# Loading all raw token weights first and decoding one piece a step, with zeros on TensorE and the cap and first keys moved ahead, in a soft-capped attention and token/channel mixer

## The chip, the cores and the metric

The kernel runs on one core of one Trainium2 chip. The metric is the device time of one execution in microseconds; the median of three runs is given with their range. Profiles show one execution, taken by the hardware profiler. TensorE (PE) multiplies matrices, VectorE (DVE), ScalarE (ACT) and GpSimd (POOL) compute on vectors, and SyncE (SP) issues most DMAs.

## The reference

Two stages: attention with soft-capped scores, then a mixer over tokens and over channels. B, H, S, D = 4, 12, 448, 64.

```python
scores = np.matmul(q, k.transpose(0, 1, 3, 2)) / np.sqrt(64)
scores = cap * np.tanh(scores / cap)
scores = scores - np.max(scores, axis=-1, keepdims=True)
attn = np.exp(scores)
attn = attn / (np.sum(attn, axis=-1, keepdims=True) + 1e-09)
x = np.matmul(attn, v)                      # then (4, 448, 768)
xt = x.transpose(0, 2, 1)
h = np.maximum(xt @ w_tok1, 0.0) @ w_tok2   # over tokens, 448 -> 256 -> 448
u = x + h.transpose(0, 2, 1)
h2 = np.maximum(u @ w_ch1, 0.0) @ w_ch2     # over channels, 768 -> 1536 -> 768
out = u + h2
```

The four weight matrices are float64 on the host and reach the kernel as raw 64-bit words. The kernel decodes them into a high and a low float32 part, and every product with them is made of three matmuls.

## The kernel before

**Attention.** The 12 heads of a batch are six pairs of heads. A pair has three full key chunks of 128 (units c = 0, 1, 2), and the remaining 64 keys of two neighbouring pairs share one packed unit (c = 3). So two pairs make seven units, in the order (p, 0..3), (p+1, 0..2), and the list of all units is worked off two units a step. In a step `scores_of` puts the score matmuls (`qk_unit`, ps_qk, two banks) on TensorE, then two tanh and two exp on ScalarE; the exps go into the tiles e, of which there are eight. Step t of the loop issues on TensorE first the products of probabilities and values of step t (`pv_full`, `pv_packed`, into ps_pv), then the scores of step t + 2. ps_pv has two banks, one a pair: a pair gets its bank with its first product, and when its four products are done, `evac` copies the bank out on VectorE in the next step. The third pair's first product comes in step 3, the fourth pair's in step 5.

VectorE also sums the probabilities: `add_up` adds the e tiles of a pair into acc (`L236`, `L242`, and two half adds `L254`). The column sums of acc go through TensorE (ps_s, L262), a gather, a reciprocal and a broadcast, and `scale_pair` (L300) writes the normalized result to u. `transpose_pair` (ps_t, L323) and the two token products (ps_h, ps_u) are given to TensorE as background work of later steps.

**Order.** Within the attention stage every engine executes its instructions in the order in which the Python code issues them (a manual schedule). `at(d, f, y)` puts off a piece of work by d steps; `run(0)`, `run(1)`, `run(2)` issue it at the beginning, the middle and the end of a step. SyncE's DMAs are in the same order too, and one that waits holds up those behind it.

**Token weights.** w1 comes in two pieces of 512 elements a partition, w2 in two of 448. `decode_steps` gives four closures, and in the first batch each step that contains a unit c = 1 starts one. `decode` issues the load of a piece into one of two wraw tiles; `lag` steps later `first` issues two VectorE operations (L98, L101), a step later `second` two more (L106, L107), then `third` two (L110, L111), and `fourth` a cast to the high part (L115) and a subtraction on GpSimd for the low part (L118).

**Start.** SP loads the first pair's queries, ScalarE's queue loads its keys and then the cap; SP goes on with the second and third pair and the values. Both tanh and exp need a factor that VectorE makes of the cap (L463 to L465).

Of the kernel before, what the change touches and what calls it, by code (L numbers as in the profile page):

```python
# [8 lines left out]
F32 = mybir.dt.float32  # L9
F32R = mybir.dt.float32r  # L10
I32 = mybir.dt.int32
# [4 lines left out]
P = 128  # L16
B, H, S, D = 4, 12, 448, 64
# [5 lines left out]
NK = 4  # L23
NF = NK - 1
NV = 2 * NF + 1
LAST = S - (NK - 1) * P
# [3 lines left out]
DU = 512  # L30
HALF = C // 2
NHALF = NC // 2
SP = 32
FREE = 40.0
EPS = 1e-9


@with_exitstack
def tile_softcap_mixer(ctx, tc, qk, v, cap, w1, w2, wc1, wc2, out):
    nc = tc.nc  # L40

    const = ctx.enter_context(tc.tile_pool(name="const", bufs=1))
    wp = ctx.enter_context(tc.tile_pool(name="wp", bufs=2))
    ps_a = ctx.enter_context(tc.tile_pool(name="ps_a", bufs=2, space=PSUM))
    ps_b = ctx.enter_context(tc.tile_pool(name="ps_b", bufs=2, space=PSUM))
    ps_c = ctx.enter_context(tc.tile_pool(name="ps_c", bufs=2, space=PSUM))

    def bits(ap):
        return ap.bitcast(F32)

    cap_sb = const.tile([P, 1], F32, name="cap_sb")
# [4 lines left out]
    u = [const.tile([P, NC, S], F32, name=f"u{b}") for b in range(B)]  # L56
# [6 lines left out]
    w1s = last_u[:, :n1].rearrange("p (x c t) -> p x c t", x=2, c=NK)  # L63
    w2s = last_u[:, n1:n1 + 2 * NT * S].rearrange("p (x t s) -> p x t s", x=2, t=NT)
# [6 lines left out]
    def at(d, f, y=0):  # L71
        later.setdefault((now[0] + d, y), []).append(f)

    def run(y):
        for f in later.pop((now[0], y), []):
            f()

    def tick(most=3):
        now[0] += 1
        for y in range(most):  # L80
            run(y)
# [4 lines left out]
    pace = [1]  # L86

    def decode(src, n, hi, lo, early, blank):
        r = wp.tile([P, 2 * DU], I32, tag="wraw", name="wraw")[:, :2 * n]
        nc.sync.dma_start(r, src.bitcast(I32))  # L90
        r = r.rearrange("p (n t) -> p n t", t=2)

        z = wp.tile([P, DU], I32, tag="wz", name="wz")[:, :n]
        zf = bits(z)

        def first():
            if early:
                nc.vector.tensor_scalar(  # L98
                    z, r[:, :, 1], 1, 1, op0=ALU.logical_shift_left, op1=ALU.logical_shift_right
                )  # L100
                nc.vector.tensor_scalar_mul(zf, zf, 2.0 ** -16)  # L101
                return
            nc.scalar.activation(zf, bits(r[:, :, 1]), AF.Abs, scale=2.0 ** -16)  # L103

        def second():
            nc.vector.tensor_scalar(zf, zf, 2.0 ** -31, 2.0 - 2.0 ** -23, op0=ALU.max, op1=ALU.min)  # L106
            nc.vector.tensor_scalar(z, z, 4, 1, op0=ALU.logical_shift_left, op1=ALU.logical_shift_right)  # L107

        def third():
            nc.vector.scalar_tensor_tensor(z, r[:, :, 1], -(1 << 31), z, op0=ALU.bitwise_and, op1=ALU.bitwise_or)  # L110
            nc.vector.scalar_tensor_tensor(z, r[:, :, 0], 29, z, op0=ALU.logical_shift_right, op1=ALU.bitwise_or)  # L111

        def fourth():
            if early:
                nc.vector.tensor_copy(hi, zf)  # L115
            else:
                nc.scalar.activation(hi, zf, AF.Copy)  # L117
            nc.gpsimd.tensor_tensor(lo, zf, hi, op=ALU.subtract)  # L118
            if blank is not None:
                nc.gpsimd.memset(bits(blank), 0.0)  # L120

        d = lag[0]
        at(d, first)
        d += slow[0]
        at(d, second, 2)
        at(d + 1, third, 2)
        at(d + 2, fourth, 2)

    def decode_steps(src, dst, n, early=False, blank=None):
        hi = dst[:, 0].rearrange("p a b -> p (a b)")  # L130
        lo = dst[:, 1].rearrange("p a b -> p (a b)")
        return [
            lambda i=i: decode(
                src[:, i:i + n], n, hi[:, i:i + n], lo[:, i:i + n], early, blank if i + n == hi.shape[1] else None
            )
            for i in range(0, hi.shape[1], n)
        ]

    def group_weights(g):
        t1, t2 = wset[g % 2]  # L140
        t1 = t1.rearrange("p (x c f) -> p x c f", x=2, c=NC)
        t2 = t2.rearrange("p (x f c) -> p x f c", x=2, f=GF)
        return (t1, t2), decode_steps(wc1[g], t1, DU) + decode_steps(wc2[g], t2, DU)
# [9 lines left out]
    def half(i, j):  # L153
        return slice((i ^ j) * D, ((i ^ j) + 1) * D)
# [3 lines left out]
    def load_pair(b, p):  # L158
        raw = pi.tile([P, 2, S], F32, tag="qkraw", name="qkraw", bufs=3)
        if b == 0 and p == 0:  # L160
            nc.sync.dma_start(raw[:, 0], qk[b, p, :, 0])
            nc.scalar.dma_start(raw[:, 1], qk[b, p, :, 1])
        else:
            nc.sync.dma_start(raw, qk[b, p])
        raws[b, p] = raw

    def load_v(b, p):
        nc.sync.dma_start(vn[p % 3], v[b, p])
# [42 lines left out]
    def pv_full(b, p, c):  # L211
        ps, first, last = pv_bank(b, p)
        for j in range(2):
            nc.tensor.matmul(  # L214
                ps[j * D:(j + 1) * D, :S], vn[p % 3][:, j * NF + c], es[b, p, c][:, j], start=first, stop=last
            )
# [179 lines left out]
    second = {}  # L396
# [53 lines left out]
        engines={engines.PE, engines.DVE, engines.Activation, engines.Pool, engines.SP}  # L450
    ))
    load_pair(*pairs[0])
    nc.scalar.dma_start(cap_sb, cap)
    nc.vector.memset(near, 0.0)
    nc.scalar.activation(near, near, AF.Exp)
    load_pair(*pairs[1])
# [7 lines left out]
    nc.vector.tensor_scalar_mul(tsc, tsc, 1.0 / D ** 0.5)  # L464
    nc.vector.tensor_scalar(near, cap_sb, -FREE, FREE, op0=ALU.max, op1=ALU.min)  # L465

    tokw_steps = decode_steps(w1, w1s, DU, True, w1s[:LAST, 1, NK - 1]) + decode_steps(w2, w2s, S, True)
    w0, w0_steps = group_weights(0)

    def scores_of(t):  # L470
# [16 lines left out]
    for t in range(steps_in):  # L487
        two = units[2 * t:2 * t + 2]
        tick(0)
        run(0)  # L490
        for b, p, c in two:
            if c < NF:
                pv_full(b, p, c)
        for b, p, c in two:
            if c == NF:
                pv_packed(b, p)
        scores_of(t + 2)
        run(1)
        for b, p, c in two:
            add_up(b, p, c)  # L500
            n = pairs.index((b, p))
            if c == (2 if p % 2 else NF) and n + 3 < len(pairs):
                at(1, lambda n=n: load_v(*pairs[n + 3]))
            if b == 0 and c == 1 and tokw_steps:
                tokw_steps.pop(0)()
            if b >= 1 and p % 2 and c == 2 and w0_steps:
                w0_steps.pop(0)()
        late = t + 2 - steps_in
        if late >= 0:
            if late == 0:  # L510
                nc.vector.tensor_scalar(
                    mag, cap_sb.bitcast(I32), 1, 1, op0=ALU.logical_shift_left, op1=ALU.logical_shift_right
                )
                in_att.close()
                m0 = ctx.enter_context(tc.tile_pool(name="m0", bufs=1, reuse_waits="tile", side="right"))
                split_tile(0, m0)
            for cc in range(3 * late, 3 * late + 3):
                split_u(0, cc)
        background(TOK / 9)
        run(2)  # L520
        for b, p, c in two:
            if p % NHALF == NHALF - 1 and c == 2:
                work.extend(tok_work(b, p // NHALF))
# [102 lines left out]
    def attend(b, h, vr):  # L626
# [5 lines left out]
        for c in range(NK):  # L632
# [7 lines left out]
            nc.vector.reduce_sum(st[:, 1:2], t, axis=mybir.AxisListType.X)  # L640
            nc.vector.tensor_scalar_add(st[:, 1:2], st[:, 1:2], EPS)
            nc.vector.reciprocal(st[:, 1:2], st[:, 1:2])
# [13 lines left out]
    def general():  # L656
        def settle():
            while later:
                tick()

        for step in decode_steps(w1, w1s, DU, False, w1s[:LAST, 1, NK - 1]) + decode_steps(w2, w2s, S):
            step()
            settle()
        given.clear()
        settled.clear()
        for b in range(B):
            for h in range(H):
                p, j = divmod(h, 2)
                if j == 0:
                    vr = bits(wp.tile([P, DU], I32, tag="wz", name="vr")).rearrange("p (j c d) -> p j c d", j=2, c=NK)  # L670
                    for i in range(2):
                        nc.sync.dma_start(vr[:, i, :NF], v[b, p, :, i * NF:(i + 1) * NF])
                        nc.sync.dma_start(vr[LAST:, i, NF], v[b, p, half(p % 2, i), NV - 1])
                attend(b, h, vr)
            work.extend(tok_work(b, 0) + tok_work(b, 1))
            while left[b] if b == B - 1 else work or running:
                background(1000, 1)
                tick()
        for b in range(B):
            for cc in range(NC):  # L680
                split_u(b, cc)
        for g in range(NG):
            w, steps = group_weights(g)
            for step in steps:
                step()
                settle()
            for b in range(B):
                ch2(w[1], b, ch1(w[0], b), g == NG - 1)
# [57 lines left out]
```

## Time and profile before

| | before |
|---|---|
| median of 3 runs | 608.33 us (607.08 to 608.47) |
| profiled execution | 606.1 us |
| its span, first to last instruction | 604.3 us |
| TensorE busy | 590.4 us, 98% |
| VectorE busy | 385.3 us, 64% |
| ScalarE busy | 254.4 us, 42% |
| GpSimd busy | 54.5 us, 9% |

The span leaves out 1.8 us of the profiled execution. The shares are means over stages that differ: attention fills roughly the first third, in which ScalarE and VectorE have much more to do than later, and the channel mixer on TensorE fills the rest. A busy time of TensorE includes stretches in which its pipelined matmuls wait for another engine, so that it has to be read beside the other engines' times of the same stretch. Lines of the profile are those of the kernel before; the changed kernel's are larger by 6 to 19.

### The profile page before, as it was taken

How to read it: one execution, taken by the hardware profiler on the slowest of the kernel's cores; microseconds unless marked ns; L12 is line 12 of the kernel's file. 1: busy time of each engine (PE TensorE's matmuls, PEld its weight loads, DVE VectorE, ACT ScalarE, POOL GpSimd, SP SyncE). 2: the span in 40 equal slices, each digit the busy share in tenths (PEclk: the TensorE clock that was granted, in tenths of full speed). 3: DMA queues.
4: the chain of work that ended last, by engine and by line, in shares of the span. 5: the costliest groups of instructions: out<-in, count | busy, mean ns of one | idle time of the engine just before them, and what ended most of it. 6: DMA issues, size and time to landing. Idle time of an engine off the chain costs nothing.

```text
span 604.3 us, 7751 instructions
## 1 busy us (share of the span) xinstructions
PE 590.4 (98%) x3008; PEld 437.3 (72%) x3008; DVE 385.3 (64%) x626; ACT 254.4 (42%) x330; POOL 54.5 (9%) x48
## 2 busy tenths in 40 slices
PE   7998999999999999999999999999999999999997
PEld 2232444444444489997998999899989999999986
DVE  2899869696996996547788386438643853333324
ACT  6998987887879733115332022012211220000000
POOL 0020000000010000002331022001200120000000
PEclk9999999999999999999999999999999999999999
DMA  6445445254442211001344121202120200000224
GB/s 202 149 143 152 143 132 160 78 157 143 130 160 82 68 31 32 0 1 36 96 120 132 36 68 57 86 0 78 63 70 1 69 2 0 1 1 0 94 100 178
DMA packets 24476, 49.12 MB, mean 81 GB/s; under 512 B 6768, under 2 KB 16368, under 8 KB 24432
## 3 DMA queue, kind: packets, MB, share of 16 engines
q1 hardware_dynamic: 24000, 48.21, 24.8%
q8 instruction: 25, 0.41, 0.3%
q10 hardware_dynamic: 432, 0.34, 0.2%
q14 instruction: 19, 0.16, 0.1%
HBM read 42.86 MB, written 5.59 MB: 80 GB/s over the span
## 4 chain that ended last, share of the span: by engine, by line
PE 82%; DVE 10%; ACT 3%; DMA 2%; issue 2%; POOL 0%; DVEq 0%; ACTq 0%; SPq 0%
PE ps_o L563 26%; PE ps_g L546 26%; PE ps_pv L214 8%; PE ps_qk L179 7%; PE ps_h L350 5%; PE ps_u L370 5%; PE ps_s L262 2%; PE ps_pv L223 2%; DMA wraw<-in_wc 1%; DVE wz L110 1%; PE ps_qk L185 1%; PE ps_t L323 1%; ACT e L192 1%; DVE u L568 1%; DVE acc L254 1%
## 5 line engine op out<-in xcount | busy, mean ns | idle before, releaser
L563 PE MATMUL ps_o<-g,wc 128*128 128x448 f32 x864 | 182.8, 367 | 0.2 <-DVE u L568 0.2
L563 PEld LDWEIGHTS ps_o<-g,wc 128*128 128x128 f32 x864 | 161.5, 188 | 15.6 <-DVE u L568 1.3
L546 PE MATMUL ps_g<-uhl,wc 128*128 128x448 f32 x648 | 138.3, 367 | 0.0
L546 PEld LDWEIGHTS ps_g<-uhl,wc 128*128 128x128 f32 x648 | 120.9, 188 | 10.3
L568 DVE TENSOR_TENSOR u<-u,ps_o 128x448 f32<-128x448 f32 (+1 forms) x145 | 86.8, 613 | 47.1 <-PE ps_o L563 46.8
L192 ACT ACTIVATE e<-ps_qk,tsc 128x896 f32<-128x896 f32 x84 | 81.1, 1023 | 28.3 <-PE ps_qk L179 22.3
L197 ACT ACTIVATE e<-e,near 128x896 f32<-128x896 f32 x84 | 83.6, 1059 | 0.0
L118 POOL TENSOR_TENSOR wc<-wz,wc 128x512 fp32r<-128x512 f32 x36 | 48.2, 1342 | 385.6 <-ACT wc L117 364.3
L551 ACT ACTIVATE g<-ps_g 128x896 fp32r<-128x896 f32 x24 | 22.0, 916 | 143.1 <-PE ps_g L546 143.1
L552 DVE SCALAR_TENSOR_TENSOR g<-ps_g,g 128x896 fp32r<-128x896 f32 x24 | 26.1, 1089 | 75.0 <-ACT g L551 75.0
L179 PE MATMUL ps_qk<-qkraw 64*128 64x448 f32 x288 | 67.6, 581 | 4.5 <-DMA qkraw<-in_qk 4.0
L214 PE MATMUL ps_pv<-e,vn 128*64 128x448 f32 x288 | 64.2, 556 | 0.4 <-ACT e L192 0.4
L179 PEld LDWEIGHTS ps_qk<-qkraw 64*128 64x128 f32 x288 | 24.4, 189 | 46.3 <-issue 13.2
L117 ACT ACTIVATE wc<-wz 128x512 fp32r<-128x512 f32 x36 | 22.6, 629 | 74.9 <-PE ps_g L546 33.9
L546 PE MATMUL ps_g<-last_u,wc 128*128 128x448 f32 x216 | 45.5, 367 | 0.7 <-PE ps_o L563 0.6
L546 PEld LDWEIGHTS ps_g<-last_u,wc 128*128 128x128 f32 x216 | 40.4, 188 | 4.8 <-issue 0.9
L103 ACT ACTIVATE wz<-wraw 128x512 f32<-128x512 f32 x36 | 24.2, 673 | 45.8 <-DMA wraw<-in_wc 30.5
L214 PEld LDWEIGHTS ps_pv<-e,vn 128*64 128x64 f32 x288 | 16.5, 135 | 33.3 <-issue 16.0
L106 DVE TENSOR_SCALAR wz<-wz 128x512 f32<-128x512 f32 (+1 forms) x40 | 17.5, 437 | 34.7 <-ACT wz L103 34.6
L350 PEld LDWEIGHTS ps_h<-wc,last_u 128*128 128x128 f32 x176 | 30.5, 188 | 8.0 <-issue 6.0
L350 PE MATMUL ps_h<-wc,last_u 128*128 128x384 f32 x176 | 36.0, 343 | 0.0
L370 PE MATMUL ps_u<-last_u,wc 128*128 128x448 f32 x144 | 34.1, 376 | 1.5 <-DVE wc L359 0.8
(48 smaller groups left out, 410.5 us busy)
## 6 DMA issues: line engine op xcount, KB each, us to landing
wraw<-in_wc SPq DMA_DIRECT2D x36, 512.0 KB, 3.5
qkraw<-in_qk SPq DMA_DIRECT2D x23, 448.0 KB, 3.4
vn<-in_v SPq DMA_DIRECT2D x24, 224.0 KB, 3.3
rb<-rs SPq DMA_DIRECT2D x48, 112.0 KB, 2.8
out_t<-u SPq DMA_DIRECT2D x23, 224.0 KB, 1.9
wraw<-in_w SPq DMA_DIRECT2D x2, 512.0 KB, 4.7
wraw<-in_w SPq DMA_DIRECT2D x2, 448.0 KB, 3.4
sums<-xs SPq DMA_DIRECT2D x48, 1.8 KB, 2.1
```

Source lines behind the costliest of these rows:

```text
L103: nc.scalar.activation(zf, bits(r[:, :, 1]), AF.Abs, scale=2.0 ** -16)
L118: nc.gpsimd.tensor_tensor(lo, zf, hi, op=ALU.subtract)
L179: nc.tensor.matmul(ps[:, j, :S], raw[r, 1, c * P:(c + 1) * P], raw[r, 0], start=True, stop=True)
L192: nc.scalar.activation(e, scores.pop((b, p, c))[:, :, :S], AF.Tanh, scale=tsc)
L197: nc.scalar.activation(e, e, AF.Exp, scale=near)
L214: nc.tensor.matmul(ps[j * D:(j + 1) * D, :S], vn[p % 3][:, j * NF + c], es[b, p, c][:, j], start=first, stop=last)
L350: nc.tensor.matmul(ps[:, :HALF], w, x, start=(n == 0), stop=(n == len(mm) - 1))
L370: nc.tensor.matmul(ps[:, :S], h1[:, hi, t, cs], w2s[:, wi, t, :], start=(n == 0), stop=(n == 3 * NT - 1))
L546: nc.tensor.matmul(ps[:, i, :S], w[:, wi, cc, fs], uhl[b][:, ui, cc, :], start=(n == 0), stop=(n == 3 * NC - 1))
L552: nc.vector.scalar_tensor_tensor(g[:, 1], ps[:, :, :S], 0.0, g[:, 0], op0=ALU.max, op1=ALU.subtract)
L563: nc.tensor.matmul(ps[:, :S], w[:, wi, i, cs], g[:, gi, i, :], start=(n == 0), stop=(n == 3 * GF - 1))
L568: nc.vector.tensor_tensor(u[b][:, cc, r], u[b][:, cc, r], ps[:, r], op=ALU.add)
```

## The change

- The four loads of raw token weights no longer go into wraw. They are issued before the first step, right behind the first three pairs' loads, into the tiles u of the third and fourth batch, which nothing else uses by then.
- `decode` with a tile for the raw data returns its four parts instead of putting them off. In each of the steps 0, 1, 2 and 3 all four parts of one piece are issued, at the end of the step.
- The first pair's keys are cut: the first 128 columns stay on ScalarE's queue, the other 320 go to SP. The cap goes to SP, right behind the queries.
- Two matmuls of zeros (128 x 128 by 128 x 384) are put ahead of the first scores on TensorE.

```diff
     def decode(src, n, hi, lo, early, blank):
-        r = wp.tile([P, 2 * DU], I32, tag="wraw", name="wraw")[:, :2 * n]
+        if early is None:
+            r = wp.tile([P, 2 * DU], I32, tag="wraw", name="wraw")[:, :2 * n]
+        else:
+            r = early.bitcast(I32)[:, :2 * n]
         nc.sync.dma_start(r, src.bitcast(I32))
...
+        if early is not None:
+            return first, second, third, fourth
         d = lag[0]
         at(d, first)
...
         if b == 0 and p == 0:
             nc.sync.dma_start(raw[:, 0], qk[b, p, :, 0])
-            nc.scalar.dma_start(raw[:, 1], qk[b, p, :, 1])
+            nc.scalar.dma_start(raw[:, 1, :P], qk[b, p, :, 1, :P])
+            nc.sync.dma_start(cap_sb, cap)
+            nc.sync.dma_start(raw[:, 1, P:], qk[b, p, :, 1, P:])
...
-    nc.scalar.dma_start(cap_sb, cap)
+    idle = ps_c.tile([P, 512], F32, tag="c", name="idle")
+    zeros = nc.const_aps.tensor(0.0, [P, HALF], F32)
+    for _ in range(WARM):
+        nc.tensor.matmul(idle[:, :HALF], zeros[:, :P], zeros, start=True, stop=True)
...
-    tokw_steps = decode_steps(w1, w1s, DU, True, w1s[:LAST, 1, NK - 1]) + decode_steps(w2, w2s, S, True)
+    room = [u[b].rearrange("p c s -> p (c s)") for b in (B - 2, B - 1)]
+    tokw_steps = [
+        step()
+        for step in decode_steps(w1, w1s, DU, room[0], w1s[:LAST, 1, NK - 1]) + decode_steps(w2, w2s, S, room[1])
+    ]
...
-            if b == 0 and c == 1 and tokw_steps:
-                tokw_steps.pop(0)()
...
+        if tokw_steps:
+            for f in tokw_steps.pop(0):
+                at(0, f, 2)
```

WARM is 2. In the changed kernel L98 to L118 are L104 to L124, the adds L236, L242 and L254 are L247, L253 and L265, the copy L276 is L287, and the products L214 and L223 are L225 and L234.

On VectorE, before, this stands from the first copy out of ps_pv (the first pair's) to the second copy (the second pair's) and the add behind it.

```order
L276 COPY xr<-ps_pv 128x448
L236 TENSOR_TENSOR acc<-e 128x896
L254 TENSOR_TENSOR acc<-acc,e 64x448 x2
L242 TENSOR_TENSOR acc<-acc,e 128x896
L106 TENSOR_SCALAR wz<-wz 128x512
L107 TENSOR_SCALAR wz<-wz 128x512
L98 TENSOR_SCALAR wz<-wraw 128x512
L101 TENSOR_SCALAR wz<-wz 128x512
L276 COPY xr<-ps_pv 128x448
L236 TENSOR_TENSOR acc<-e 128x896
```

Ahead of the first copy stand only L98 and L101 of the first piece. In the changed kernel this leads up to the second copy (u_78 is the tile of the fourth batch with the raw w2).

```order
L121 CAST last_u<-wz 128x448
L253 TENSOR_TENSOR acc<-acc,e 128x896
L104 TENSOR_SCALAR wz<-u_78 128x448
L107 TENSOR_SCALAR wz<-wz 128x448
L112 TENSOR_SCALAR wz<-wz 128x448
L113 TENSOR_SCALAR wz<-wz 128x448
L116 SCALAR_TENSOR_TENSOR wz<-u_78,wz 128x448
L117 SCALAR_TENSOR_TENSOR wz<-u_78,wz 128x448
L121 CAST last_u<-wz 128x448
L287 COPY xr<-ps_pv 128x448
L247 TENSOR_TENSOR acc<-e 128x896
```

The whole fourth piece, and further up the other three, now stand ahead of the second copy; two pieces stand ahead of the first one. From the fifth step on VectorE has no decoding of token weights.

On SP, before, the program begins so (vn are the values, wraw<-in_w the token weights).

```order
L161 DMA qkraw<-in_qk 128x448
L164 DMA qkraw<-in_qk 128x896
L168 DMA vn_95<-in_v 128x448
L164 DMA qkraw<-in_qk 128x896
L168 DMA vn_96<-in_v 128x448
L168 DMA vn_97<-in_v 128x448
L164 DMA qkraw<-in_qk 128x896
L90 DMA wraw<-in_w 128x1024
L164 DMA qkraw<-in_qk 128x896
```

And in the changed kernel.

```order
L170 DMA qkraw<-in_qk 128x448
L172 DMA cap_sb<-in_cap 128x1
L173 DMA qkraw<-in_qk 128x320
L175 DMA qkraw<-in_qk 128x896
L179 DMA vn_95<-in_v 128x448
L175 DMA qkraw<-in_qk 128x896
L179 DMA vn_96<-in_v 128x448
L179 DMA vn_97<-in_v 128x448
L94 DMA u_77<-in_w 128x1024 x2
L94 DMA u_78<-in_w 128x896 x2
L175 DMA qkraw<-in_qk 128x896 x2
```

All token weights now stand ahead of the fourth pair's load, and the cap and most of the first keys ahead of the second pair's.

## Rows read from the trace of the kernel before

**Rows 1.** Stretch: length, busy us of PE, PEld, DVE, ACT, POOL, clock, DMA share, GB/s.
```profile
10.00:20.00 10.00, 10.00 (x50) 2.81 (x48) 6.91 (x10) 10.00 (x12) 0.00 (x0) 1.00 0.54 187
...
40.00:50.00 10.00, 9.56 (x56) 2.90 (x52) 9.72 (x15) 10.00 (x12) 1.80 (x2) 1.00 0.53 165
```

**Rows 2.** Timeline of the start: start us, length us, engine, line, what, [idle before].
```profile
1.19 0.46 ACTq L453 DMA_DIRECT2D cap_sb<-in_cap  x1
...
4.01 3.34 PE L179 MATMUL ps_qk<-qkraw 64*128 64x448 f32 x8 [4.01 <-DMA qkraw<-in_qk]
...
6.31 0.16 DVE L463 RECIPROCAL tsc<-cap_sb 128x1 f32<-128x1 f32 x1 [5.44 <-DMA cap_sb<-in_cap]
...
6.76 1.91 ACT L192 ACTIVATE e<-ps_qk,tsc 128x896 f32<-128x896 f32 x2 [3.60 <-DVE near L465]
...
10.56 1.09 DVE L236 TENSOR_TENSOR acc<-e 128x896 f32<-128x896 f32 x1 [3.83 <-ACT e L197]
```

**Rows 3.** Timeline: scores and tanh of step 5, products of step 5, scores and tanh of step 7.
```profile
22.45 0.98 PE L185 MATMUL ps_qk<-qkraw 64*64 64x448 f32 x8
...
25.01 1.93 ACT L192 ACTIVATE e<-ps_qk,tsc 128x896 f32<-128x896 f32 x2
...
28.86 0.97 PE L214 MATMUL ps_pv<-e,vn 128*64 128x448 f32 x4
...
30.67 1.77 PE L179 MATMUL ps_qk<-qkraw 64*128 64x448 f32 x8
...
32.30 1.96 ACT L192 ACTIVATE e<-ps_qk,tsc 128x896 f32<-128x896 f32 x2
```

**Rows 4.** VectorE's groups, 10 to 60 us: busy us, mean ns of one | idle before.
```profile
L236 DVE TENSOR_TENSOR acc<-e 128x896 f32<-128x896 f32 x7 | 7.6, 1080 | 5.0 <-ACT e L197 4.9
L254 DVE TENSOR_TENSOR acc<-acc,e 64x448 f32<-64x448 f32 x12 | 7.4, 619 | 0.4
L276 DVE COPY xr<-ps_pv 128x448 f32<-128x448 f32 x6 | 3.7, 618 | 0.0
...
L107 DVE TENSOR_SCALAR wz<-wz 128x512 int32<-128x512 int32 x2 | 1.8, 902 | 0.1
L111 DVE SCALAR_TENSOR_TENSOR wz<-wraw,wz 128x512 int32<-128x512 int32 x2 | 1.4, 692 | 0.1
L110 DVE SCALAR_TENSOR_TENSOR wz<-wraw,wz 128x512 int32<-128x512 int32 x2 | 1.4, 684 | 0.0
L111 DVE SCALAR_TENSOR_TENSOR wz<-wraw,wz 128x448 int32<-128x448 int32 x2 | 1.3, 627 | 0.1
...
L101 DVE TENSOR_SCALAR wz<-wz 128x512 f32<-128x512 f32 x2 | 0.9, 428 | 0.1
...
L106 DVE TENSOR_SCALAR wz<-wz 128x512 f32<-128x512 f32 x2 | 0.8, 420 | 0.0
L101 DVE TENSOR_SCALAR wz<-wz 128x448 f32<-128x448 f32 x2 | 0.8, 394 | 0.1
```

**Rows 5.** Timeline around the first transposes.
```profile
52.31 2.08 ACT L197 ACTIVATE e<-e,near 128x896 f32<-128x896 f32 x2
...
53.14 1.10 PE L323 MATMUL ps_t<-ident,u 128*128 128x128 f32 x8 [1.87 <-DVE u L300]
...
54.17 1.72 PE L214 MATMUL ps_pv<-e,vn 128*64 128x448 f32 x8
```

**Rows 6.** DMA issues: what, queue, count, KB each, median us to landing.
```profile
sums<-xs SPq DMA_DIRECT2D x48, 1.8 KB, 2.1
```

**Rows 7.** Columns as in rows 1: two stretches of 1 us.
```profile
9.00:10.00 1.00, 1.00 (x10) 0.20 (x4) 0.00 (x0) 1.00 (x2) 0.00 (x0) 1.00 0.01 5
...
12.00:13.00 1.00, 1.00 (x8) 0.30 (x4) 0.00 (x0) 1.00 (x2) 0.00 (x0) 1.00 1.06 423
```

**Rows 8.** Timeline, 41 us: a subtraction on GpSimd beside a VectorE operation.
```profile
41.08 1.36 POOL L118 TENSOR_TENSOR last_u<-wz,last_u 128x512 fp32r<-128x512 f32 x1 [8.39 <-DVE last_u L115]
41.33 1.35 DVE L107 TENSOR_SCALAR wz<-wz 128x448 int32<-128x448 int32 x1
```

More of the change, by code (lines that the diff above doesn't have):

```diff
@@ L35 @@
 EPS = 1e-9
+WARM = 2
 @with_exitstack
@@ L88, in decode @@
     def decode(src, n, hi, lo, early, blank):
-        r = wp.tile([P, 2 * DU], I32, tag="wraw", name="wraw")[:, :2 * n]
+        if early is None:
+            r = wp.tile([P, 2 * DU], I32, tag="wraw", name="wraw")[:, :2 * n]
+        else:
+            r = early.bitcast(I32)[:, :2 * n]
         nc.sync.dma_start(r, src.bitcast(I32))
         r = r.rearrange("p (n t) -> p n t", t=2)
-        z = wp.tile([P, DU], I32, tag="wz", name="wz")[:, :n]
-        zf = bits(z)
+        z = zf = None
         def first():
-            if early:
+            nonlocal z, zf
+            z = wp.tile([P, DU], I32, tag="wz", name="wz")[:, :n]
+            zf = bits(z)
+            if early is not None:
                 nc.vector.tensor_scalar(
@@ L113, in fourth @@
         def fourth():
-            if early:
+            if early is not None:
                 nc.vector.tensor_copy(hi, zf)
@@ L120, in fourth @@
                 nc.gpsimd.memset(bits(blank), 0.0)
+        if early is not None:
+            return first, second, third, fourth
         d = lag[0]
@@ L127, in decode, with decode_steps @@
         at(d + 2, fourth, 2)
-    def decode_steps(src, dst, n, early=False, blank=None):
+    def decode_steps(src, dst, n, room=None, blank=None):
         hi = dst[:, 0].rearrange("p a b -> p (a b)")
@@ L133, in decode_steps @@
             lambda i=i: decode(
-                src[:, i:i + n], n, hi[:, i:i + n], lo[:, i:i + n], early, blank if i + n == hi.shape[1] else None
+                src[:, i:i + n], n, hi[:, i:i + n], lo[:, i:i + n],
+                None if room is None else room[:, 2 * i:], blank if i + n == hi.shape[1] else None
             )
@@ L659, in settle @@
                 tick()
-        for step in decode_steps(w1, w1s, DU, False, w1s[:LAST, 1, NK - 1]) + decode_steps(w2, w2s, S):
+        for step in decode_steps(w1, w1s, DU, None, w1s[:LAST, 1, NK - 1]) + decode_steps(w2, w2s, S):
             step()
```

## The prediction

> **What bounds the kernel now.** I read the busy times by stretch first. From 10 to 50 us ScalarE is busy 10.00 of every 10.00 us [rows 1], the first and the last of four such stretches; TensorE shows the same only because its records are stretched while it waits. So the attention steps are paced by ScalarE: a step (two tanh, two exp) starts every 3.65 us. Call the steps 0, 1, 2 and so on; step 0 starts with the first tanh at 6.76 and step 7 with the tanh at 32.30 [rows 2, 3], and (32.30 - 6.76) / 7 = 3.65. A ScalarE that is never idle cannot make up a loss. From about 55 us TensorE carries the token mixing too and is the bound; what is lost or won before that moves the end by as much.
>
> The timeline of the start comes next. TensorE's first matmuls wait 4.01 us for data, but the first tanh waits longer: the cap's issue at 1.19 ends only at 6.31, where VectorE's reciprocal starts, and tanh starts at 6.76 [rows 2]. Last come VectorE's groups and the two places where TensorE waits for it: the copies out of the ps_pv banks and the transposes [rows 3, 4, 5].
>
> **The start.** The cap moves from ScalarE's queue, behind 224 KB, to SP's, behind 224 KB, and the keys are cut so that the first matmul needs 288 KB and not 448. The cap lands at 6.31 if nothing changes, and no sooner than 1.2 + 2.1 = 3.3, by the landing of the 1.8 KB gather [rows 6]. The first matmul starts at 4.01 with all 448 KB landed, so I let the query half be there at about 3.8 and the cap just behind it, near 4.3; with the 0.45 us from reciprocal to tanh that gives 4.75. The first scores are then late. The first eight records took 3.34 us, the same eight later 1.77 [rows 2, 3]: TensorE starts at half its pace. The two zero matmuls are four records of 384 columns; at the cold 0.83 us for 448 columns that is 4 x 0.71 = 2.9 us, from 0.8 to 3.7, so they just fit ahead of the data. If the real scores still run cold, unit 0 is ready at 4.0 + 1.7 = 5.7 and unit 1 at 7.3, which for the paced phase is worth a start of 6.4; if warm, 4.95. I take 5.3, which is 1.5 us gained, between 0 and 2.0.
>
> **The loads.** 1.97 MB of token weights now stand in SP's queue ahead of the fourth pair's keys. The first loads have ended by 9 us (5 GB/s are left in 9 to 10), and the engines reach 423 GB/s [rows 7]. Hence the first 512 KB land near 9.0 + 1.2 = 10.3, all four by 14, the fourth pair by about 15; TensorE wants that pair after step 3's second product, near 21. Every load finds its cover; nothing is added here.
>
> **VectorE's queue.** This is the term that decides. A decoding is six operations and a cast. Before, its parts are spread over several steps, and six of its instructions stand ahead of the second copy out of ps_pv; now all four pieces, 28 instructions, stand ahead of it. VectorE runs in order. The copy frees the bank that TensorE's products of step 5 need (the third and fourth pair use the two banks of the first and second), and so they wait for it.
>
> The price of a 512-wide piece, with L98 and an undisturbed L107 taken as long as L101: 3 x 0.428 + 2 x 0.420 + 0.684 + 0.692 = 3.50 us, the cast taken as long as L106; of a 448-wide one: 4 x 0.394 + 2 x 0.627 and a cast taken as 0.39, 3.2 us [rows 4]. The usual work between the first decoding and the end of the second copy is three adds of 1.08, four half adds of 0.62 and two copies of 0.62, 6.9 to 7.0 us. Together 2 x 3.50 + 2 x 3.2 + 7.0 = 20.4 us.
>
> GpSimd's subtraction after each cast comes on top: while one ran from 41.08 for 1.36 us, L107 took 1.35 us where its form takes 0.43, so VectorE lost 0.92 [rows 8]. The mean of 902 ns for the 512-wide L107 shows it once in two [rows 4]. Three subtractions fall into the queue: 2.7 us; their bounds are 0, if the adds that now stand behind the cast are not held up as L107 was, and 3 x 1.36 = 4.1. I take 2.7. The Trainium skill ("SBUF — State Buffer", section "Who interferes with whom") says that a VectorE instruction with two SBUF inputs is blocked, too, by a GpSimd one that reads SBUF; the adds are such. The L107 row agrees for its kind; on adds no row here rests. By that rule the sum stays; without it, 2.7 us go.
>
> When does the queue start? The first add began 3.80 us after the first tanh (10.56 against 6.76 [rows 2]), so at 9.1, and ends at 10.2; the first weights land at 10.3. The second copy ends at 10.3 + 20.4 + 2.7 = 33.4. The products that wait for it began at 28.86 before [rows 3], so with the earlier start they would be due at 27.4: VectorE is 6.0 us late. Behind them on TensorE stand the scores of step 7. They start 1.81 us later (28.86 to 30.67) and the first of the two units takes half of 1.77 [rows 3], so step 7's tanh starts at 33.4 + 1.8 + 0.9 = 36.1 in place of 32.30: **3.8 us later than before**, the early start already in it. The first copy is late as well: 10.3 + 3.50 + 1.08 + 1.24 + 0.9 + 3.50 + 0.62 = 21.1, and the half of step 3's products that needs it, 0.9 us ahead of the scores at 22.45, would be due at 20.1. But those scores, 1.0 us long, are done 1.6 us before ScalarE asks for them at 25.01 [rows 3], which covers 1.0 us.
>
> After that VectorE has no decoding left. Its backlog is then 8 us of adds and copies against steps of 3.65 us with some 2.9 us of work each; by my sum the copies for steps 7 and 8 end just as they are wanted, and the pace of 3.65 us is back from step 7.
>
> **What the later steps win.** Before, the decoding in steps 9 to 12 made VectorE late, and the first transposes waited 1.87 us for u. Not all of this is to be had: the products behind the transposes began at 54.17, but their first half needs an exp that ends at 52.31 + 1.04 = 53.35, the second one that ends at 54.39; with VectorE on time they end at about 55.25 and not 55.83 [rows 5]. So 0.6 us are won, between 0 and 1.87.
>
> **The sum.** 3.8 - 0.6 = +3.2 us, on the profiled execution 606.1 + 3.2 = 609.3. The median of the runs, 608.33, stands 2.2 above that execution, so the forecast is 608.33 + 3.2 = **611.5 us**. Its own range: start as before +1.4, subtractions between half and all of 1.36 each, credit between 0 and 1.87: +1.2 to +5.2, 609.5 to 613.5.
>
> **Rivals.**
> *The subtractions cost VectorE nothing.* Then the copy ends at 30.7, step 7 starts at 33.4, and +1.1 - 0.6 = +0.5 us remain: 608.8. For it: no row shows an add held up as L107 was. Against it: one row's operation tripled.
>
> *VectorE keeps up.* The rows of L101 and L106 are times of one instruction, and neighbours that do not depend on each other overlap. If the queue from 10.3 to the end of the second copy took under 17.8 us (due time 27.4, plus 0.7 us that the scores are ahead of ScalarE), the copy would not be felt, and the 1.5 us of the start and the 0.6 of the transposes would be kept: -2.1 us, **606.2, faster**. It would need 23.1 us of queue to shrink by 5.3, and the decoding works in place, each operation on the one before. This is also what it would look like if the change did what its parts suggest.
>
> *TensorE falls back to half pace.* The column sums, which stand just ahead of the late products, wait for an add that ends 0.9 + 3.2 + 0.6 = 4.7 us before the second copy does, and take half a microsecond more; then TensorE idles 4.2 us in one piece. The products and the first scores behind it, 2.7 us, would take twice that: +5.9 us, 614.2. For it: the first records after 4.01 us of idle took twice their time [rows 2]. Against: after the 1.87 us gap at the transposes the products kept their pace [rows 5]. The Trainium skill ("TensorE: Matmul & The Clock Gate", section "Why this matters for your kernels") advises against idle gaps between bursts, since the clock falls to half; by it 614.2 would be the time. No row here shows a fall in mid-kernel.
>
> **How the numbers follow.** Forecast 64%, free subtractions 13%, VectorE keeping up 10%, half pace 13%. About 0.3%, 1.8 us, is what a measurement of this kernel can tell from no change. Slower by more: 61 of the forecast's 64 and all of the half pace, 74%. Within: 3 + 13 + 2, 18%. Faster: 8%. The range takes in all but the case of keeping up and the far ends of the others: 608.5 to 614.5.
>
> **What would show it.** In the changed profile VectorE should be busy without a break from about 10 to 35 us; TensorE should wait some 4 us for VectorE ahead of 33.4, at the products (L225) with the copy (L287) as releaser, and a little ahead of the column sums (L273); ScalarE should be idle about 5 us ahead of the tanh near 36; the transposes' wait for u should be gone. The first tanh near 5.3 tests the start, L265 or L247 longer than their form beside L124 the subtractions. If ScalarE shows no gap between 20 and 40 us, the argument is wrong and the time is near 606.

## The result, and the profile after

The changed kernel takes 613.78 us (median of 6 runs, 611.46 to 614.80) against 607.05 us for the kernel before (6 runs, 606.36 to 608.47): a ratio of 1.0102, 95% interval 1.0078 to 1.0125. It is 6.7 us slower. Its profiled execution took 614.06 us with a span of 612.3 us, 8.0 us more than the span of the one before.

Busy times by stretch (us, then the busy us of PE, PEld, DVE, ACT and POOL, then the granted clock of TensorE, DMA share and GB/s) show where to look. They answer to [rows 1], where ScalarE was busy all the time and the clock stood at 1.00:

```profile
20.00:25.00 5.00, 2.88 (x15) 0.70 (x16) 4.83 (x8) 4.48 (x5) 1.58 (x2) 0.87 0.01 3
25.00:30.00 5.00, 5.00 (x26) 1.55 (x20) 4.78 (x10) 3.47 (x4) 0.57 (x1) 0.79 0.40 138
30.00:35.00 5.00, 1.73 (x14) 0.28 (x10) 4.79 (x9) 4.06 (x5) 1.64 (x2) 0.89 0.29 92
35.00:40.00 5.00, 4.74 (x16) 1.47 (x18) 4.85 (x7) 0.00 (x0) 0.84 (x1) 0.50 0.00 0
```

ScalarE, which cannot make up a loss, has nothing to do from 35 to 40 us. VectorE is busy almost without a break (4.78 to 4.85 of 5). TensorE's granted clock is at its lower level, 0.50, all through the last of these stretches; the 0.87, 0.79 and 0.89 of the other three mean that it was there for a part of each.

The timeline of the start (start, length, engine, line, what, [idle time before]) answers to [rows 2]:

```profile
3.77 4.00 PE L190 MATMUL ps_qk<-qkraw 64*128 64x448 f32 x12
3.93 0.16 DVE L477 RECIPROCAL tsc<-cap_sb 128x1 f32<-128x1 f32 x1 [3.06 <-DMA cap_sb<-in_cap]
...
5.03 0.74 PEld L190 LDWEIGHTS ps_qk<-qkraw 64*128 64x128 f32 x4 [0.75 <-DMA qkraw<-in_qk]
5.69 1.01 ACT L203 ACTIVATE e<-ps_qk,tsc 128x896 f32<-128x896 f32 x1 [3.01 <-PE ps_qk L190]
...
6.99 1.01 ACT L203 ACTIVATE e<-ps_qk,tsc 128x896 f32<-128x896 f32 x1 [0.29 <-PE ps_qk L190]
...
11.69 0.43 DVE L104 TENSOR_SCALAR wz<-u 128x512 int32<-128x512 int32 x1 [0.71 <-DMA u<-in_w]
```

The cap is there at 3.93 instead of 6.31, and the first tanh begins at 5.69 instead of 6.76. The second one waits 0.29 us for scores, so the paced steps are only 0.67 us earlier: step 1's tanh starts at 9.76 and not at 10.43. VectorE's first decoding waits for its data until 11.69.

The timeline from 15 to 41 us holds the two late copies (L287). It answers to [rows 3]:

```profile
15.50 2.05 POOL L124 TENSOR_TENSOR last_u<-wz,last_u 128x512 fp32r<-128x512 f32 x1 [14.12 <-DVE last_u L121]
...
16.53 2.14 DVE L265 TENSOR_TENSOR acc<-acc,e 64x448 f32<-64x448 f32 x2
...
22.34 0.62 DVE L287 COPY xr<-ps_pv 128x448 f32<-128x448 f32 x1
...
22.51 1.28 POOL L124 TENSOR_TENSOR last_u<-wz,last_u 128x512 fp32r<-128x512 f32 x1 [4.96 <-DVE last_u L121]
22.88 1.85 DVE L247 TENSOR_TENSOR acc<-e 128x896 f32<-128x896 f32 x1
...
23.06 1.20 PE L225 MATMUL ps_pv<-e,vn 128*64 128x448 f32 x4 [2.12 <-ACT e L203]
...
24.19 1.77 PE L196 MATMUL ps_qk<-qkraw 64*64 64x448 f32 x8
...
26.05 1.01 ACT L203 ACTIVATE e<-ps_qk,tsc 128x896 f32<-128x896 f32 x1 [1.58 <-PE ps_qk L196]
...
29.43 1.92 POOL L124 TENSOR_TENSOR last_u<-wz,last_u 128x448 fp32r<-128x448 f32 x1 [5.28 <-DVE last_u L121]
...
30.27 1.33 DVE L104 TENSOR_SCALAR wz<-u 128x448 int32<-128x448 int32 x1
...
30.77 0.96 PE L273 MATMUL ps_s<-acc,ones 128*32 128x448 f32 x8
...
34.55 0.62 DVE L287 COPY xr<-ps_pv 128x448 f32<-128x448 f32 x1
...
35.27 1.76 PE L225 MATMUL ps_pv<-e,vn 128*64 128x448 f32 x4 [3.53 <-issue]
...
36.95 1.77 PE L234 MATMUL ps_pv<-e,vn 64*64 64x448 f32 x8
...
38.66 2.79 PE L190 MATMUL ps_qk<-qkraw 64*128 64x448 f32 x8
...
40.57 1.01 ACT L203 ACTIVATE e<-ps_qk,tsc 128x896 f32<-128x896 f32 x1 [6.51 <-PE ps_qk L190]
```

Read it from the bottom. Step 7's tanh starts at 40.57, not at 32.30, after 6.51 us in which ScalarE waits for scores. The scores (38.66) stand behind step 5's products (35.27). Those begin 0.10 us after the second copy ends (34.55 + 0.62 = 35.17). The trace puts the 3.53 us before them down to "issue", and the 2.12 us at 23.06 to ScalarE's e; but the exps that those products read had ended at 18.83 + 1.99 = 20.82, and what ends just before the products restart is both times the copy, at 22.96 and 35.17. The products and scores behind the second wait take about twice their time: 1.77 us for L234 x8, where L185 x8, the same form, took 0.98 [rows 3].

Stretches of 1 us show when the clock went (columns as above):

```profile
23.00:24.00 1.00, 0.94 (x4) 0.23 (x4) 1.00 (x1) 1.00 (x2) 0.94 (x2) 0.84 0.00 0
24.00:25.00 1.00, 1.00 (x7) 0.31 (x8) 0.97 (x2) 0.48 (x1) 0.15 (x1) 0.50 0.06 16
...
33.00:34.00 1.00, 0.00 (x0) 0.00 (x0) 0.97 (x2) 1.00 (x2) 0.00 (x0) 0.96 0.32 126
34.00:35.00 1.00, 0.00 (x0) 0.00 (x0) 0.97 (x3) 0.06 (x1) 0.29 (x1) 0.50 0.00 0
...
40.00:41.00 1.00, 1.00 (x6) 0.34 (x2) 0.97 (x2) 0.43 (x1) 0.00 (x0) 0.63 0.02 2
```

Behind the first wait the clock falls between 23 and 24 us, when TensorE is at work again, and is back at 1.00 in the stretch from 28 us. Ahead of the second wait TensorE's last matmul (L273) ended at 31.73. Near 34 us the clock falls from 2.4 to 1.2 GHz, while TensorE is still idle, and it is back at full speed in the stretch from 41 us.

The transposes answer to [rows 5]:

```profile
59.54 1.09 PE L334 MATMUL ps_t<-ident,u 128*128 128x128 f32 x8
...
60.56 1.72 PE L225 MATMUL ps_pv<-e,vn 128*64 128x448 f32 x8
```

The wait for u is gone. What was +8.3 us at step 7 is +6.4 us here (59.54 against 53.14).

### The profile page after: what moved, and what is told of

Same layout as the page of the kernel before. It is cut to its first block, busy times and chain, and to the rows that moved or that the text cites. A ratio compares the mean times of both kernels' runs of the same rounds, so it can differ in the third digit from the quotient of the medians.

```text
span 612.3 us, 7763 instructions
## 1 busy us (share of the span) xinstructions
PE 597.0 (98%) x3012; PEld 439.9 (72%) x3012; DVE 385.9 (63%) x626; ACT 254.7 (42%) x330; POOL 55.6 (9%) x48
## 4 chain that ended last, share of the span: by engine, by line
PE 80%; ACT 9%; DVE 6%; issue 2%; DMA 2%; POOL 0%; DVEq 0%; ACTq 0%; SPq 0%; POOLq 0%
PE ps_g L565 26%; PE ps_o L582 25%; PE ps_qk L190 7%; PE ps_pv L225 6%; PE ps_h L361 5%; PE ps_u L381 5%; ACT e L203 4%; ACT e L208 3%; PE ps_pv L234 2%; PE ps_s L273 1%; PE ps_qk L196 1%; PE ps_t L334 1%; DMA wraw<-in_wc 1%; DVE wz L116 1%; DVE u L587 1%
## 5 line engine op out<-in xcount | busy, mean ns | idle before, releaser
L565 PEld LDWEIGHTS ps_g<-uhl,wc 128*128 128x128 f32 x648 | 120.9, 188 | 10.3
L124 POOL TENSOR_TENSOR wc<-wz,wc 128x512 fp32r<-128x512 f32 x36 | 48.2, 1341 | 419.1 <-ACT wc L123 393.5
L225 PE MATMUL ps_pv<-e,vn 128*64 128x448 f32 x288 | 65.0, 562 | 5.7 <-issue 3.5
L225 PEld LDWEIGHTS ps_pv<-e,vn 128*64 128x64 f32 x288 | 16.8, 136 | 38.6 <-issue 20.9
```

Source lines behind the costliest of these rows:

```text
L225: nc.tensor.matmul(ps[j * D:(j + 1) * D, :S], vn[p % 3][:, j * NF + c], es[b, p, c][:, j], start=first, stop=last)
L565: nc.tensor.matmul(ps[:, i, :S], w[:, wi, cc, fs], uhl[b][:, ui, cc, :], start=(n == 0), stop=(n == 3 * NC - 1))
```

## The experiments

The theory: what costs the time is the order on VectorE, all four pieces ahead of the second copy; GpSimd's subtractions and TensorE's clock each add some microseconds to it; the start and the early loads do no harm. The rivals are that loading 1.97 MB early delays the start, that the zeros or the cap's new queue hurt, that the subtractions are free, and that a whole piece is too much in any step.

**Only the order undone.** Loads first and the new start stay; the parts of a piece are spread over the steps as before.

```diff
+            if b == 0 and c == 1 and tokw_steps:
+                f = tokw_steps.pop(0)
+                at(2, f[0])
+                at(3, f[1], 2)
+                at(4, f[2], 2)
+                at(5, f[3], 2)
-        if tokw_steps:
-            for f in tokw_steps.pop(0):
-                at(0, f, 2)
```

> The changed kernel, but each piece of the token weights is decoded in four parts over steps, at the same places as in the kernel before; the loads first, the cap, the cut keys and the zeros stay. Theory (the order of the decoding is the whole loss): VectorE's two copies come in time again, no wait of TensorE at step 3's or step 5's products, and the time is that of before less the start's 0.7 to 1.1 us: about 606.2 us. Rival (the loads ahead of the fourth pair, the zeros or the cap's new place cost something): it stays above 608.

Measured: 606.40 us (the kernel before, measured beside it: 607.29), ratio 0.9979 [0.9966, 0.9993]. The loss is gone and a small gain is there. From the timeline of its profiled execution, the slowest of its 12 runs (608.83 us):

```profile
6.00 3.36 PE L190 MATMUL ps_qk<-qkraw 64*128 64x448 f32 x8 [0.44 <-DMA qkraw<-in_qk]
...
7.91 1.01 ACT L203 ACTIVATE e<-ps_qk,tsc 128x896 f32<-128x896 f32 x1 [1.30 <-PE ps_qk L190]
```

The second copy ends at 24.07, step 7's tanh starts at 32.56. The copies are in time; step 7 is even so 0.26 us later than before, since in this execution the rest of the first keys came only at 6.00, the second tanh began at 7.91, and the gain of the start was lost. The gain is in the times and not in this trace. So the order makes the whole loss, 1.0102 against 0.9979, about 7.5 us.

**Only the start done.** The kernel before with the cap on SP's queue, the cut keys and the zeros.

```diff
-            nc.scalar.dma_start(raw[:, 1], qk[b, p, :, 1])
+            nc.scalar.dma_start(raw[:, 1, :P], qk[b, p, :, 1, :P])
+            nc.sync.dma_start(cap_sb, cap)
+            nc.sync.dma_start(raw[:, 1, P:], qk[b, p, :, 1, P:])
...
-    nc.scalar.dma_start(cap_sb, cap)
+    idle = ps_c.tile([P, 512], F32, tag="c", name="idle")
+    zeros = nc.const_aps.tensor(0.0, [P, HALF], F32)
+    for _ in range(WARM):
+        nc.tensor.matmul(idle[:, :HALF], zeros[:, :P], zeros, start=True, stop=True)
```

> The kernel before with the start alone changed (cap and cut keys on SP, two zero matmuls). Theory: tanh starts about 1 us earlier and the second tanh 0.7, ScalarE is then never idle, so 606.2 us, the same as e1. If e1 is slower than this one, the difference is the price of loading all raw weights first. Rival: the early start is lost again before the transposes, 607 us.

Measured: 606.26 us (607.29), ratio 0.9976 [0.9961, 0.9991]. Its timeline:

```profile
5.67 1.01 ACT L195 ACTIVATE e<-ps_qk,tsc 128x896 f32<-128x896 f32 x1 [2.99 <-PE ps_qk L182]
7.05 1.01 ACT L195 ACTIVATE e<-ps_qk,tsc 128x896 f32<-128x896 f32 x1 [0.37 <-PE ps_qk L182]
...
52.52 1.10 PE L326 MATMUL ps_t<-ident,u 128*128 128x128 f32 x8 [1.88 <-DVE u L303]
```

The gain of the start is kept: in this execution the transposes begin 0.62 us earlier than in [rows 5], with the same wait. With and without the early loads the ratio is the same within its interval, so the loads cost nothing that shows; the intervals, 0.0014 either way, leave room for some 1 us.

**The two waits of TensorE filled.** The changed kernel with products of zeros put ahead of the products of steps 3 and 5, three in step 3 and four in step 5. They go into the banks of the second and of the third pair, which are in use there, and add zero. VectorE's order is untouched.

```diff
+        for _ in range({3: 3, 5: 4}.get(t, 0)):
+            nc.tensor.matmul(
+                pvp[0, {3: 1, 5: 2}[t]][:, :HALF], zeros[:, :P], zeros, start=False, stop=False
+            )
```

> The changed kernel with TensorE kept at work in its two waits: three zero matmuls ahead of step 3's products and four ahead of step 5's, each adding zero to a bank in use. VectorE's queue is the same. Theory (about 2.6 us of the loss are records at half pace after the waits): the granted clock stays 1.00 from 20 to 42 us, step 7's tanh starts near 38 in place of 40.6 and the time is about 611.2 us. Rival (the pace after the waits is not on the path): 613.8 us as before, though the clock stays up.

Measured: 611.46 us (607.29), ratio 1.0057 [1.0036, 1.0078]. From its timeline:

```profile
31.56 2.86 PE L510 MATMUL ps_pv<-const-float32-0.0 128*128 128x384 f32 x8
...
34.83 0.61 DVE L287 COPY xr<-ps_pv 128x448 f32<-128x448 f32 x1
...
38.43 1.91 ACT L203 ACTIVATE e<-ps_qk,tsc 128x896 f32<-128x896 f32 x2 [5.56 <-PE ps_qk L190]
```

The granted clock is 1.00 in every stretch of 5 us from 20 to 40. The copy ends at 35.44, no earlier than without the zeros; from there to step 7's tanh it takes 2.99 us where the changed kernel took 40.57 - 35.17 = 5.40. The half pace is therefore 2.4 us of the loss in the trace, and 1.0102 - 1.0057 or 2.7 us in the times. More than half of the loss is left: the late copy.

**No subtractions.** The changed kernel without GpSimd's subtractions for the token weights: the low parts of w1 and w2 are left out (set to zero at the start).

```diff
-            nc.gpsimd.tensor_tensor(lo, zf, hi, op=ALU.subtract)
-            if blank is not None:
-                nc.gpsimd.memset(bits(blank), 0.0)
+            if early is None:
+                nc.gpsimd.tensor_tensor(lo, zf, hi, op=ALU.subtract)
+                if blank is not None:
+                    nc.gpsimd.memset(bits(blank), 0.0)
...
+    for low in (w1s, w2s):
+        nc.gpsimd.memset(bits(low[:, 1]), 0.0)
```

> The changed kernel without GpSimd's four subtractions for the token weights; the low parts are set to zero at the start instead, so that part of the computation is left out. Theory (the subtractions hold VectorE up by 2.6 us ahead of the second copy): L265, L247 and L104 are back at 1.25, 1.09 and 0.39 us, the copy ends 2.6 us earlier, near 32.6, and the time is 611.2 us, or 609 if TensorE's waits get too short for its clock to fall. Rival (they cost VectorE nothing that counts): 613.8 us.

Measured: 609.43 us (607.29), ratio 1.0041 [1.0023, 1.0059]. From its timeline:

```profile
22.81 1.76 PE L226 MATMUL ps_pv<-e,vn 128*64 128x448 f32 x4 [2.23 <-ACT e L204]
23.75 1.25 DVE L266 TENSOR_TENSOR acc<-acc,e 64x448 f32<-64x448 f32 x2
...
33.30 0.97 PE L226 MATMUL ps_pv<-e,vn 128*64 128x448 f32 x4 [1.92 <-ACT e L209]
...
35.12 1.77 PE L191 MATMUL ps_qk<-qkraw 64*128 64x448 f32 x8
...
36.19 1.91 ACT L204 ACTIVATE e<-ps_qk,tsc 128x896 f32<-128x896 f32 x2 [2.48 <-PE ps_qk L191]
```

The adds are back at their usual length, 1.25 us for two halves where the changed kernel had 2.14 beside L124; of the three rows there that were held up ahead of the second copy, L265 lost 0.89 us, L247 0.76 and L104 0.94 against the lengths here (1.25, 1.09 and 0.39), 2.6 us in all. The queue from the first decoding to the second copy's end is 12.34 to 33.20, 20.9 us against 23.5. TensorE waits only 1.92 us before the products of step 5, its clock stays at full there, and step 7's tanh is at 36.19. The subtractions so cost 2.6 us directly. By the times they cost 1.0102 - 1.0041 or 3.7 us; that the other 1.1 us is the clock, which a longer wait of TensorE brings down, fits this trace but is not shown by itself. The clock went both ways in this kernel: five of its ten runs have a mean of 1.000 (607.97 to 610.36 us), five of 0.994 to 0.996 (609.08 to 611.84), among these the profiled one, in which it fell behind the wait of 2.23 us.

**A group in each step.** The changed kernel with each piece cut into three groups (first part; second; third and fourth), one in each of steps 0 to 11.

```diff
+    tokw_parts = [fs for f in tokw_steps for fs in (f[:1], f[1:2], f[2:])]
...
-        if tokw_steps:
-            for f in tokw_steps.pop(0):
+        if tokw_parts:
+            for f in tokw_parts.pop(0):
                 at(0, f, 2)
```

> The changed kernel, with its loads first and its new start, but each of the four pieces cut into three groups of instructions (the first part; the second; the third and fourth) and one group queued in each of steps 0 to 11, instead of a whole piece in each of steps 0 to 3. Theory (the whole loss is the order on VectorE: four pieces ahead of the second copy out of the ps_pv bank): with five groups ahead of the second copy no copy is late, and nine groups instead of eleven stand ahead of the scaling that the first transposes wait for, so that the transposes' wait of 1.9 us goes as well: 607.3 - 1.0 (start) - 1.7 = 604.6 us, between 604.0 and 605.3. Rival (VectorE is busy without a pause to 60 us, so what is taken from the transposes' wait returns at another one): only the start is gained, 606.3 us. A second rival (a group in every step makes the copies late again): above 607.3 us.

Measured: 604.69 us (604.24 to 604.99; before 607.75), ratio 0.9940 [0.9927, 0.9953]. This is faster than both kernels. From its timeline:

```profile
49.41 1.09 PE L334 MATMUL ps_t<-ident,u 128*128 128x128 f32 x8
...
50.43 1.72 PE L225 MATMUL ps_pv<-e,vn 128*64 128x448 f32 x8
...
51.16 2.09 ACT L208 ACTIVATE e<-e,near 128x896 f32<-128x896 f32 x2
```

The transposes do not wait, and start 3.73 us earlier than in [rows 5]; 1.13 us of this is the start in this execution (step 1's tanh at 9.30 and not at 10.43), 1.87 us the wait, and most of the rest a wait of 0.44 us that TensorE had ahead of its products at 48.44 and has no more. The products behind them start before the exp of 51.16, so they cannot need it; this matters for what the later steps win, below.

**The same with a gap.** No group in steps 8 to 11; the last four come in steps 12 to 15.

```diff
-        if tokw_parts:
+        if not 8 <= t < 12 and tokw_parts:
```

> As the kernel with a group in each step, but no group in steps 8 to 11: the last four groups come in steps 12 to 15, so eight groups stand ahead of the scaling before the first transposes. Theory: the transposes' wait is gone in any case and the adds of steps 8 to 11 are early; what is gained over the kernel without the gap is whatever wait was left there, 0 to 0.5 us: 604.3 us. Rival: the last groups now meet the second pair's copies and the products that need the second token weights, and cost 1 us or more: 605.6 us or above.

Measured: 604.63 us (607.75), ratio 0.9937 [0.9924, 0.9950]. No different from the kernel without the gap: there was no wait left to take, and the groups do no harm later either.

**A whole piece in every second step.**

```diff
-        if tokw_steps:
+        if t % 2 == 0 and tokw_steps:
```

> The changed kernel with a whole piece in steps 0, 2, 4 and 6 instead of 0, 1, 2 and 3, so that a piece still goes into VectorE's queue in one lump, but two instead of four stand ahead of the second copy. Theory (what counts is how much work stands ahead of the copy, two pieces less are 6.4 us of VectorE's own and 1.3 us under GpSimd's subtraction, 7.7 us): the second copy ends near 35.2 - 7.7 = 27.5 us, which is its due time, step 7's tanh comes near 32 us and TensorE's clock stays at full; all twelve groups stand ahead of the transposes' scaling, so their wait is 1.9 us and up to 1.5 us more: 606.3 to 608 us, 607.3 us. Rival (a whole piece in one step is itself too much, wherever it stands, as each delays the adds and the copy of its step): the copies are late by some 2 us each and TensorE idles four times: 610 us or more.

Measured: 606.97 us (607.75), ratio 0.9985 [0.9973, 0.9997]. The time is as the theory said, and so are the first two copies: the second ends at 26.91. The rival falls: it wanted all four copies late and 610 us or more. But the way to that time was another. From its timeline:

```profile
42.84 0.62 DVE L287 COPY xr<-ps_pv 128x448 f32<-128x448 f32 x1
...
43.51 0.97 PE L234 MATMUL ps_pv<-e,vn 64*64 64x448 f32 x4 [1.12 <-DVE xr L287]
...
45.48 1.90 ACT L203 ACTIVATE e<-ps_qk,tsc 128x896 f32<-128x896 f32 x2 [2.91 <-PE ps_qk L190]
```

The fourth piece, queued in step 6, makes the fourth copy late; TensorE waits 1.12 us and ScalarE 2.91. (The third copy, which ends at 35.97, is a little late too: TensorE waits 0.99 us and goes on at 36.08, 0.11 us behind it, and ScalarE does not feel it.) The steps are then 2.2 us later than before (45.48 against 43.24), which gives VectorE the time that it lacked at the transposes, and these do not wait. I had expected the wait to stay at the transposes and to grow. It is the same work on VectorE; it is charged where its queue first meets someone who waits.

**No zeros at the start.** The kernel with the start alone, WARM = 0.

> The kernel before with the edits of the start alone, and without the four products of zeros on TensorE. Theory (the start's gain is the earlier cap, and the zeros bring little, since the kernel before shows its first eight score products at the same pace without them): first tanh near 5.7 us, second near 7.4 instead of 7.05 us, 606.3 to 606.7 us. Rival (the zeros are what makes the first scores early): the gain is gone, 607.3 us.

Measured: 607.28 us (607.75), ratio 0.9996 [0.9981, 1.0011]; a miss. Its trace is near the theory: the first tanh is at 5.71, the second at 7.20, the transposes at 52.80, 0.34 us earlier than in [rows 5] and 0.28 later than with the zeros. But its times show no gain that can be told from none. The interval overlaps that of the start with zeros (0.9961 to 0.9991); by the ratios the two are 1.2 us apart. One trace of each cannot settle it: step 1's tanh starts at 9.98 without the zeros, and in the eight traces with them anywhere from 9.30 to 10.68. The zeros' worth stays open.

## Why the prediction was right, and where its sizes were not

The direction, the place and the mechanism were right: VectorE's queue makes the second copy late, step 7 starts late, ScalarE's time is lost, and nothing later makes up for it. The forecast was 611.5 us, 3.2 us over the three runs shown then; the time is 613.8, inside the range, and 6.7 us over the six runs of before. The clock's fall, set apart as a rival at 13%, is what came: the likeliest case as I had it, with TensorE at full pace, did not. That the time lies so near the forecast is therefore in part luck. A change of +6.7 us is twice the +3.2 of the forecast and beyond the +1.2 to +5.2 of that case; the range holds it because it was drawn up to 614.5 to take in the half pace (+5.9 us, 614.2), and because the median of the three runs on which it stands is 1.3 us above that of the six. Point by point:

- **VectorE's queue.** Forecast 23.1 us from the first decoding to the second copy's end, measured 35.17 - 11.69 = 23.5. The three subtractions were put at 2.7 us and cost 2.6; the rows of the changed kernel show adds and a decoding held up, and the run without them shows it. The Trainium skill ("SBUF — State Buffer", section "Who interferes with whom") has this blocking for VectorE instructions with two SBUF inputs; the trace agrees for adds, which go from 1.25 to 2.14 us. The prediction says that no row shows an add held up. The trace of the kernel before has one, later than the stretches of the prediction:

```profile
60.63 1.13 POOL L118 TENSOR_TENSOR last_u<-wz,last_u 128x448 fp32r<-128x448 f32 x1 [8.42 <-DVE last_u L115]
...
61.12 1.75 DVE L254 TENSOR_TENSOR acc<-acc,e 64x448 f32<-64x448 f32 x2
```

Two half adds took 1.75 us beside a subtraction, where two of 619 ns [rows 4] take 1.25. The rival of free subtractions, at 13%, had this row against it.

- **The landing of the first weights.** Forecast 10.3, measured 11.69 (11.68 to 12.34 in the other traces in which VectorE waits for it): 1.4 us too early. I sized it from the gap in the transfers after 9 us [rows 7] and a rate of 423 GB/s; the loads stand in one queue behind the others, and the engines moved 340 GB/s from 5 to 10 us and 388 from 10 to 15.
- **The clock.** This is the term that I left out of the sum. From the copy's end to the tanh I took 2.7 us, and it took 5.4. I had one gap of 1.87 us that kept its pace [rows 5] and one of 4.0 us that did not [rows 2], and weighed a gap of 4.2 us by the first rather than by the second. A gap that comes so near to the one that is known to be slow should have gone into the likeliest case. The Trainium skill ("TensorE: Matmul & The Clock Gate", section "Why this matters for your kernels") advises against such gaps; the prediction cites it and the trace agrees at the wait of 3.53 us; in these runs the clock fell behind shorter waits too, of 2.12 and 2.23 us.
- **Step 7 in sum.** 32.30 + 3.8 was forecast, 1.4 (landing) + 0.4 (queue) + 2.7 (clock) come on top: 40.6, as measured.
- **The first copy.** Forecast 1.0 us late and covered. It ended at 22.96, 2.9 us after its due time of 20.1, because the queue began 1.4 us late and took 0.5 us longer; TensorE fell to half pace here too, and ScalarE was idle for 1.58 and 0.48 us. None of this reaches step 7, which waits for the second copy anyway: with TensorE kept at work in this wait VectorE's queue takes the same 23.5 us (11.96 to 35.44).
- **What the later steps win.** Forecast 0.6 us, measured 8.27 - 6.40 = 1.87, the whole wait. The step that failed is my reading of who the products behind the transposes wait for: I took them for those of the exps at 52.31. In the kernel with a group in each step the same products start at 50.43, ahead of the exp of their neighbourhood at 51.16; the loop's order says so too, as it puts the products of a step ahead of the scores of two steps later. By the column sums behind the transposes 0.7 us have been given back (+7.1 us: 64.64 against 57.53), so that 1.2 us of the 1.87 are kept there.
- **The start.** Forecast 1.5 us, measured 0.67. The cap came earlier than I said, at 3.93; the scores were what was late, their first unit still at half pace after the zeros (tanh at 5.69) and the second waiting for the rest of its keys until 5.03. Neither is the same in each execution. In the eight traces with this start and the zeros the rest of the keys comes between 4.75 and 6.53, the first tanh starts between 4.91 and 5.74 and step 1's between 9.30 and 10.68; against the 10.43 of the one trace of before that is from 0.25 us lost to 1.13 won, 0.6 in the mean. What decides it is open. By the times of the two kernels that have the new start and the old order it is worth 0.21 to 0.24%, some 1.4 us, with intervals from 0.07 to 0.39%.

The sum with the sizes as measured is 3.8 + 1.4 + 0.4 + 2.7 - 1.87 = +6.4 at the transposes, against +6.7 in the medians. The 8.0 us between the two spans are larger: +7.1 stands at the column sums, and the remaining 0.9 us build up after that, in stages that the edit does not touch; which of it is chance in these two executions is open.

## What to carry to other kernels

Count what stands in an in-order engine's queue ahead of the one instruction that frees a buffer, not the engine's share of the time: the same decoding behind the same start gave ratios of 1.010, 0.998 or 0.994 by its order alone. When such a wait makes TensorE idle for microseconds, put the half pace of the work behind it into the sum. Where loads can be had early at no cost, use them to spread the work that follows more evenly, here one group a step, rather than to do it as soon as possible.

## What the runs showed of the hardware

The same wait of 1.87 us at the transposes did not have the same effect in each execution. In [rows 5] the clock stayed at full. In the profiled execution of the kernel with only the order undone it fell behind that wait (the timeline, then stretches of 1 us):

```profile
53.41 1.10 PE L334 MATMUL ps_t<-ident,u 128*128 128x128 f32 x8 [1.87 <-DVE u L311]
...
54.44 3.11 PE L225 MATMUL ps_pv<-e,vn 128*64 128x448 f32 x8
```

```profile
52.00:53.00 1.00, 0.00 (x0) 0.00 (x0) 1.00 (x2) 1.00 (x2) 0.48 (x1) 1.00 0.79 301
...
54.00:55.00 1.00, 1.00 (x7) 0.47 (x7) 1.00 (x2) 1.00 (x3) 0.00 (x0) 0.81 0.09 7
55.00:56.00 1.00, 1.00 (x6) 0.41 (x4) 0.96 (x3) 0.62 (x2) 0.00 (x0) 0.50 0.00 0
```

The products took 3.11 us where [rows 5] has 1.72. Other waits of TensorE in these traces: behind 2.12, 2.23 and 3.53 us it ran at half pace, behind 1.12 and 1.92 us at full. So waits of nearly the same length went both ways. Five of the 12 runs of that kernel show a mean granted clock of 0.997, at 606.7 to 608.8 us, the other seven 0.999 to 1.000 at 605.2 to 607.3. The two fastest kernels, which have no wait at the transposes, show 0.999 or 1.000 in all of their 11 runs, within 603.3 to 605.3 us; so does the kernel with a whole piece in every second step, which has none either, in its ten, within 605.9 to 608.9. That part of what the two gain is this fall without an occasion is likely and not shown: one trace alone shows where the clock fell.
